# Bucketed attention and two dense blocks on one core: later bucket products and value halves for the second batch

## The chip, the core and the metric

One NeuronCore of a Trainium2 chip runs the whole program. The metric is the device time of one execution in microseconds (us), the median of several runs. TensorE (PE in the rows) does the matrix products into PSUM, VectorE (DVE), ScalarE (ACT) and GpSimd (POOL) the elementwise work, and SyncE (SP) issues all transfers that matter here, among them the transposing ones. Each engine takes its instructions in the order of its own queue.

## What is computed

Attention in which a query sees only the keys of its own bucket, and then two dense blocks on the result. Two batches of 8 heads, 768 positions, 64 channels; the blocks have 512 and 2048 channels.

```python
q_bits = (np.einsum('bhsd,dk->bhsk', q, proj) > 0)      # 6 bits each, the same for k
mask = q_bucket[:, :, :, None] == k_bucket[:, :, None, :]
scores = np.where(mask, scale * np.matmul(q, k.transpose(0, 1, 3, 2)), -1000000000.0)
attn = np.exp(scores - np.max(scores, axis=-1, keepdims=True))
attn_out = np.matmul(attn / (np.sum(attn, axis=-1, keepdims=True) + 1e-09), v)
x = attn_out.transpose(0, 2, 1, 3).reshape(B * S, H * D)
h = x @ w_in;    x = np.where(h > 0.0, h, np.exp(np.minimum(h, 0.0)) - 1.0) @ w_out
h = x @ w_in2;   out = (s * np.maximum(h, 0.0) ** 2 + b) @ w_out2
```

## The kernel before

Numbers are kept as pairs of 16-bit halves, a high one and a low one, so that each product is made of several. The attention runs in 96 **units**: unit `u` is 128 queries of one head against all 768 keys. Units 0 to 47 are the first batch, 48 to 95 the second; 8 units, one for each head, make a chunk of 128 positions, and two heads make a **pair** (0 to 3) that is prepared together. Unit 48 + 2p is the first that needs pair p of the second batch.

A unit has these steps: scores `s` on TensorE (`u_s`, L358), minimum over the row and scaling on VectorE and the exponential on ScalarE (`u_soft`, L368 to L370), the split of the probabilities into halves `ph`, by ScalarE (L389) and a subtraction on GpSimd (L392), a transposing transfer to `pt` (L394), and the product with the values, `xacc` (`u_av`, L412), some units later: `nxt["lag"]` lets the scores run five units ahead. Between the steps of the units stand the products of the first dense block, `h` and `x2p` (L531), which the outer loop deals out by a running credit. That block works on two chunks at a time, and only needs chunks that the attention has finished.

A pair of the second batch is prepared by steps that the function `attention` calls after the softmax of a given unit, from the table `sched`, in the order of the entries. For pair `p`, with `e1 = 41 + 2p`:

- `p_load` fetches k, q and v (`LOAD1`, `LOADV1`);
- `p_split` at `e1` makes the halves of k and q and issues three transposing transfers;
- `p_bits` at `e1 + 3` multiplies k and q by the projection (`pbit`, 14 small products, L320), compares with zero on VectorE (`bits`, L323) and copies a part of k (L326);
- `p_buck` at `e1 + 4` turns the bits into 64 further channels of k and q, by which a query and a key of different buckets get a very low score. For k and for q: two products `pone` on TensorE (L333) and two pieces on ScalarE, which read PSUM and write k or q (L337). Then the pair is ready;
- `p_v` at `PV1[p]` makes the halves of v: the high one on ScalarE (L303), the low one on VectorE (L304).

The second batch has for `s`, `pbit` and `pone` one pool of two PSUM tiles in turn (`NS = 2`), and for `ph`, the halves of k and q and `bits` one ring of four buffers (`NPH` and one of `EX`).

The order in this text is a priority, not the order of the queues. The framework (`TileContext` with a simulated timeline) goes through the program with times of its own and gives each engine, at each moment of that timeline, the ready instruction that was traced first. The queues it writes are then fixed: on the chip an engine waits for the next instruction of its queue even if a later one could run.

Of the kernel before, what the change touches and what calls it, by code (L numbers as in the profile page):

```python
# [41 lines left out]
WST = 2  # L42
LOAD1 = [30, 41, 42, 44]
LOADV1 = [46, 46, 48, 48]
PV1 = [48, 49, 50, 52]

GUEST = [(0, "k"), (0, "q"), (2, "k"), (2, "q"), (0, "v"), (1, "v")]
NS = 2
# [19 lines left out]
def model_kernel(tc, q, k, v, proj, w_in, w_out, w_in2, w_out2, s2, b2, sel, pop, eye, out):  # L68
# [24 lines left out]
    with ExitStack() as base:  # L93
# [350 lines left out]
        def at(step, fn, *a):  # L444
            sched.setdefault(step, []).append((fn, a))
# [10 lines left out]
        for hp in range(HP):  # L456
            at(PV0 + hp, p_v, 0, hp)
            e1 = (C - 1) * H + 2 * hp + 1
            at(LOAD1[hp], p_load, 1, hp, "k")
            at(LOAD1[hp], p_load, 1, hp, "q")  # L460
            at(e1, p_split, 1, hp, "k", "act")
            at(e1, p_split, 1, hp, "q", "act")
            at(e1 + 3, p_bits, 1, hp)
            at(e1 + 4, p_buck, 1, hp)
            at(LOADV1[hp], p_load, 1, hp, "v")
            at(PV1[hp], p_v, 1, hp)
        done_chunks = [0]
# [512 lines left out]
```

## Time and profile before

| | us |
|---|---|
| median of 3 runs (713.94 to 717.16) | 716.36 |
| profiled execution | 715.27 |
| its span, first to last instruction | 713.5 |
| TensorE matmul busy | 659.6 |
| VectorE busy | 516.6 |
| ScalarE busy | 417.2 |
| GpSimd busy | 272.7 |

Rows of time read: start in us, duration in us, engine, line, operation, output <- inputs, shape, count, and in brackets the idle time of the engine just before with what released it. `PEclk` is the clock that TensorE was granted as a share of the full one; a share of 0.50 is 1.2 GHz.

### The profile page before, as it was taken

The numbers are of one execution on the slowest core, as the hardware profiler recorded it, in microseconds if no ns is written. First come the engines' busy times: TensorE is split into PE (matmuls) and PEld (weight loads), VectorE is DVE, ScalarE is ACT, GpSimd is POOL, SyncE is SP. The second block draws the span as 40 slices with busy tenths as digits, with TensorE's granted clock in tenths as the row PEclk, the third lists the DMA queues.
The fourth block names the chain that finished last, engine by engine and source line by source line (L and its number), as shares of the span: only waits on it lengthen the run. The fifth ranks groups of instructions, "written<-read, shape, count | busy, mean of one in ns | idle before, by whom it ended". The sixth has DMA issues, their size and how long they took to land.

```text
span 713.5 us, 15214 instructions
## 1 busy us (share of the span) xinstructions
PE 659.6 (92%) x6192; PEld 504.0 (71%) x6192; DVE 516.6 (72%) x885; ACT 417.2 (58%) x687; POOL 272.7 (38%) x219
## 2 busy tenths in 40 slices
PE   2789869888887999999999999999999999999998
PEld 0368657676666777888888988874444446888887
DVE  5688899888878468645744699439999726999730
ACT  2897679874797887756755333234555525555520
POOL 1257778873445278945854421311211200000000
PEclk9999979999999999999999999999999999999999
DMA  9984599999899588966768545004453000000100
GB/s 234 259 222 135 159 223 225 205 229 219 178 208 215 88 142 159 154 119 123 123 112 120 132 153 175 1 25 125 121 149 115 0 1 1 16 30 32 45 30 30
DMA packets 206742, 89.73 MB, mean 126 GB/s; under 512 B 171856, under 2 KB 203344, under 8 KB 206672
## 3 DMA queue, kind: packets, MB, share of 16 engines
q1 hardware_dynamic: 206080, 88.63, 56.4%
q8 instruction: 48, 0.79, 0.5%
q10 hardware_dynamic: 592, 0.14, 0.1%
q14 instruction: 22, 0.18, 0.1%
HBM read 43.13 MB, written 3.15 MB: 65 GB/s over the span
## 4 chain that ended last, share of the span: by engine, by line
PE 59%; DMA 11%; ACT 10%; DVE 7%; issue 6%; POOL 5%; SPq 0%; DVEq 0%; ACTq 0%; POOLq 0%
PE h L531 24%; PE y L775 15%; PE x2p L531 10%; DMA pt<-ph 6%; PE s L358 4%; POOL ph L392 3%; ACT p L370 3%; PE xacc L412 3%; ACT ph L389 2%; PE xacc L406 1%; DVE e L546 1%; DMA k<-src 1%; ACT gh L551 1%; PE pT L379 1%; DVE p L368 1%
## 5 line engine op out<-in xcount | busy, mean ns | idle before, releaser
L392 POOL TENSOR_TENSOR ph<-p,ph 128x768 f16<-128x768 f32 x80 | 133.9, 1679 | 65.3 <-ACT ph L389 45.7
L531 PE MATMUL h<-x,wih 128*128 128x256 f16 x768 | 132.5, 276 | 0.1
L531 PE MATMUL h<-x,wi 128*128 128x512 f16 x576 | 124.5, 379 | 0.0
L368 DVE TENSOR_SCALAR_CACHE_REDUCE p<-s 128x768 f32<-128x768 f32 x96 | 91.0, 950 | 44.4 <-PE s L358 42.1
L370 ACT ACTIVATE p<-p,mx 128x768 f32<-128x768 f32 x96 | 89.1, 928 | 46.4 <-DVE mx L369 40.5
L775 PE MATMUL y<-wqh,a 128*128 128x256 f16 x672 | 110.3, 273 | 0.0
L775 PEld LDWEIGHTS <-a 128*128 128x128 f16 x1008 | 98.5, 98 | 11.8
L531 PE MATMUL x2p<-gh,woh 128*128 128x256 f16 x384 | 104.8, 274 | 2.0 <-ACT woh L188 1.0
L531 PE MATMUL x2p<-gh,wol 128*128 128x256 f16 x384 | 105.0, 274 | 1.5 <-DVE wol L204 1.5
L531 PE MATMUL h<-x,wil 128*128 128x256 f16 x384 | 106.0, 276 | 0.0
L531 PE MATMUL x2p<-gl,woh 128*128 128x256 f16 x384 | 104.9, 274 | 0.5 <-POOL gl L554 0.4
L531 PEld LDWEIGHTS <-wi 128*128 128x128 f16 x576 | 56.3, 98 | 67.8
L775 PE MATMUL y<-wql,a 128*128 128x256 f16 x336 | 91.2, 273 | 0.0
L358 PE MATMUL s<-k,q 128*128 128x512 f16 (+1 forms) x384 | 81.0, 336 | 4.8 <-DVE p L368 4.5
L531 PEld LDWEIGHTS <-woh 128*128 128x128 f16 x768 | 74.8, 98 | 13.5 <-ACT woh L188 1.4
L531 PEld LDWEIGHTS <-wih 128*128 128x128 f16 x768 | 75.2, 99 | 12.8 <-issue 0.5
L554 POOL TENSOR_TENSOR gl<-g,gh 128x512 f16<-128x512 f32 x48 | 58.1, 1211 | 63.3 <-ACT gh L551 62.7
L412 PE MATMUL xacc<-vv,pt 128*128 128x64 f16 x1440 | 57.7, 195 | 18.2 <-DMA pt<-ph 18.2
L412 PEld LDWEIGHTS <-pt 128*128 128x128 f16 x1440 | 53.9, 99 | 24.3 <-DMA pt<-ph 21.2
L389 ACT ACTIVATE ph<-p 128x768 f16<-128x768 f32 x80 | 66.6, 836 | 5.2 <-DMA pt<-ph 4.1
L567 DVE SCALAR_TENSOR_TENSOR g<-h,sbs,r 128x512 f32<-128x512 f32 x48 | 35.7, 745 | 23.6 <-ACT r L564 23.6
L564 ACT ACTIVATE r<-h 128x512 f32<-128x512 f32 x48 | 28.2, 590 | 39.5 <-PE h L531 39.5
(121 smaller groups left out, 1043.3 us busy)
## 6 DMA issues: line engine op xcount, KB each, us to landing
wraw<-in_moe_w_in SPq DMA_DIRECT2D x32, 512.0 KB, 3.8
wraw<-in_moe_w_out SPq DMA_DIRECT2D x32, 512.0 KB, 3.9
out<-y SPq DMA_DIRECT2D x10, 256.0 KB, 2.0
raw<-in_k SPq DMA_DIRECT2D x6, 384.0 KB, 4.4
raw<-in_q SPq DMA_DIRECT2D x6, 384.0 KB, 4.4
v<-in_v SPq DMA_DIRECT2D x4, 384.0 KB, 5.1
pt<-ph SPq DMA_TRANSPOSE x80, 4.0
x<-in_k SPq DMA_DIRECT2D x2, 384.0 KB, 5.0
```

Of the source, the lines that this page charges most:

```text
L358: nc.tensor.matmul(p[:, a0:a1], w[b, hp][:, j, c, :], kf[:, a0:a1], start=(x == 0), stop=(x == 1))
L368: nc.vector.tensor_scalar(f, sps.pop(u), CLAMP, None, op0=ALU.min, op1=ALU.min, accum_out=mx)
L370: nc.scalar.activation(out=f, in_=f, func=ACTF.Exp, scale=-sm / (SQ * SQ), bias=mx, accum_out=sums[b, c][:, h:h + 1])
L379: nc.tensor.transpose(p[:, 128 * cc:128 * cc + 128], f[:, 128 * cc:128 * cc + 128], ident)
L389: nc.scalar.activation(out=t[:, 0, :], in_=f, func=ACTF.Copy)
L392: nc.gpsimd.tensor_tensor(out=t[:, 1, :], in0=f, in1=t[:, 0, :], op=ALU.subtract)
L412: nc.tensor.matmul(acc, o[:, C * x + cc, :], vv[:, j, cc, y, :], start=(z == 0 and cc == 0), stop=(z == 2 and cc == C - 1))
L531: nc.tensor.matmul(p, ws[a](kk), xs[b](kk), start=(kk == 0 and z == 0), stop=(kk == n_kk - 1 and z == 2))
L554: nc.gpsimd.tensor_tensor(out=gl, in0=t["g"], in1=gh, op=ALU.subtract)
L564: nc.scalar.activation(out=t["r"], in_=p, func=ACTF.Relu, scale=UN)
L567: nc.vector.scalar_tensor_tensor(out=g, in0=p, scalar=sb["s"], in1=t["r"], op0=ALU.mult, op1=ALU.mult)
L775: nc.tensor.matmul(p, a[:, xa, kk, :], wq[y][:, WQ[n], kk, :], start=first and k == 0, stop=k == 3 * K2 - 1, skip_group_check=True)
```

## The change

The bucket products of a pair of the second batch (`p_buck`) are called two units behind its bit products, not one: at units 46, 48, 50 and 52 where it was 45, 47, 49 and 51. The halves of v (`p_v`) are made at units 48, 50, 52 and 54 where it was 48, 49, 50 and 52. Within a unit the entries keep the order of the pairs, so that unit 48 now has the halves of v of pair 0, the bucket products of pair 1 and the bit products of pair 2; unit 50 those of pairs 1, 2 and 3; unit 52 the halves of pair 2 and the bucket products of pair 3; and unit 54 the halves of pair 3. Loads, splits and bit products stay at their units.

```diff
 LOADV1 = [46, 46, 48, 48]
-PV1 = [48, 49, 50, 52]
+PV1 = [48, 50, 52, 54]
+BUCK1 = 5
...
             at(e1 + 3, p_bits, 1, hp)
-            at(e1 + 4, p_buck, 1, hp)
+            at(e1 + BUCK1, p_buck, 1, hp)
             at(LOADV1[hp], p_load, 1, hp, "v")
             at(PV1[hp], p_v, 1, hp)
```

## Rows read from the trace of the kernel before

**Rows 1.** The page: TensorE in 40 slices, and the chain that ended last

```profile
PE   2789869888887999999999999999999999999998
...
PE 59%; DMA 11%; ACT 10%; DVE 7%; issue 6%; POOL 5%; SPq 0%; DVEq 0%; ACTq 0%; POOLq 0%
```

**Rows 2.** Windows: length, busy us by engine, PEclk, DMA share, GB/s

```profile
200.00:260.00 60.00, 53.31 (x593) 41.34 (x591) 39.48 (x75) 49.66 (x79) 29.61 (x20) 0.97 0.83 159
260.00:300.00 40.00, 38.90 (x515) 32.93 (x513) 30.39 (x64) 32.42 (x59) 35.02 (x25) 1.00 1.01 161
300.00:400.00 100.00, 99.80 (x1251) 86.25 (x1250) 53.76 (x114) 59.40 (x100) 59.09 (x41) 1.00 0.68 117
400.00:714.00 314.00, 309.06 (x2262) 220.70 (x2259) 227.30 (x320) 131.90 (x207) 35.08 (x23) 1.00 0.21 65
```

**Rows 3.** Waits of TensorE, 200 to 260: total us, times, longest

```profile
PE xacc L412 <- DMA pt<-ph: 4.4, 5, 1.3
PE pone L333 <- DVE bits L323: 2.3, 1, 2.3
```

**Rows 4.** Windows around the wait for bits

```profile
228.60:230.90 2.30, 0.00 (x0) 0.00 (x0) 2.30 (x3) 0.34 (x1) 2.30 (x2) 1.00 0.53 153
230.90:234.10 3.20, 3.17 (x14) 1.89 (x14) 2.49 (x6) 0.63 (x1) 0.60 (x1) 0.50 1.12 139
234.10:240.00 5.90, 5.90 (x76) 4.62 (x74) 1.98 (x5) 5.83 (x9) 1.64 (x1) 0.98 0.20 44
```

**Rows 5.** Timeline of TensorE, 224 to 238

```profile
224.32 0.27 PE L320 MATMUL pbit<-k,pjk1l 128*32 128x256 f16 x1
...
228.33 0.27 PE L531 MATMUL x2p<-gl,woh 128*128 128x256 f16 x1
230.93 0.80 PE L333 MATMUL pone<-bits,sel_sb 128*128 128x512 f16 x2 [2.33 <-DVE bits L323]
231.52 0.42 PE L531 MATMUL x2p<-gh,wol 128*128 128x256 f16 x1
...
237.06 0.81 PE L358 MATMUL s<-k,q 128*128 128x512 f16 x4
```

**Rows 6.** Timeline of VectorE, 225 to 231

```profile
225.97 0.72 DVE L326 COPY k<-k 64x768 f16<-64x768 f16 x1 [2.07 <-DMA k<-srcl]
226.73 3.27 DVE L304 SCALAR_TENSOR_TENSOR vv<-x,vv 128x768 f16<-128x768 f32 x2
229.93 0.94 DVE L323 TENSOR_SCALAR bits<-pbit 128x768 f16<-128x768 f32 x1
```

**Rows 7.** Timeline of ScalarE, 233 to 239

```profile
233.47 0.93 ACT L370 ACTIVATE p<-p,mx 128x768 f32<-128x768 f32 x1 [4.53 <-DVE mx L369]
...
234.52 1.80 ACT L337 ACTIVATE k<-pone,pop_sb 64x768 f16<-64x768 f32 x2
...
237.09 1.80 ACT L337 ACTIVATE q<-pone,pop_sb 64x768 f16<-64x768 f32 x2
```

**Rows 8.** L304, 180 to 262: ns min/median/max; and GpSimd's timeline

```profile
L304 DVE SCALAR_TENSOR_TENSOR vv<-x,vv x2: 958/1679/2400, 226.7 to 227.6; 128x768 f16<-128x768 f32 x2
L304 DVE SCALAR_TENSOR_TENSOR vv<-raw,vv x2: 957/958/958, 232.4 to 239.7; 128x768 f16<-128x768 f32 x2
...
226.97 4.53 POOL L392 TENSOR_TENSOR ph<-p,ph 128x768 f16<-128x768 f32 x2 [0.49 <-ACT ph L389]
```

**Rows 9.** Timeline of TensorE: scores of units 52 and 54

```profile
247.13 0.81 PE L358 MATMUL s<-k,q 128*128 128x512 f16 x4
...
250.36 0.81 PE L358 MATMUL s<-k,q 128*128 128x512 f16 x4
```

**Rows 10.** Timelines: a wait of VectorE for a buffer, two of TensorE

```profile
206.43 1.43 DVE L265 SCALAR_TENSOR_TENSOR srcl<-x,src 128x384 f16<-128x384 f32 x2 [1.51 <-DMA pt<-ph]
...
219.10 0.55 PE L412 MATMUL xacc<-vv,pt 128*128 128x64 f16 x13 [1.35 <-DMA pt<-ph]
...
242.56 0.52 PE L412 MATMUL xacc<-vv,pt 128*128 128x64 f16 x12 [0.85 <-DMA pt<-ph]
```

**Rows 11.** Timeline of TensorE, first pairs, first batch

```profile
20.26 0.61 PE L320 MATMUL pbit<-k,pjkhl 128*32 128x512 f16 x2 [3.22 <-ACT k L337]
```

## The prediction

> **What bounds the kernel now.** I read the page first: TensorE is the engine with the most work, and the chain that ended last lies on it for 59% of the span [rows 1]. The reader is to see in the 40 slices that it is nearly full from about 240 us on and not before. Next the long stretches: from 300 to 400 us TensorE is idle for 0.2 of 100 us, from 400 to 714 for 4.9 of 314, most of that the tail, from 260 to 300 for 1.1 of 40, but from 200 to 260 for 6.7 of 60 [rows 2]. The change touches units 45 to 54, and these run in that stretch. So the kernel is bound by TensorE's work plus the holes in it, and a hole closed in 200 to 260 is kept, since what follows is full. A hole there needs only one cause: TensorE takes its instructions in the order of its queue, and x2p products that could run stand behind the one that waits.
>
> Then TensorE's waits of that stretch: 4.4 us in five waits for transposed probabilities (DMA), and 2.3 us in one wait for `bits` [rows 3]. The change speaks to the second. It lies at 228.60 to 230.93, and the 3.2 us behind it ran at a granted clock of 0.50, the lower of the two levels (1.2 GHz), with x2p products of 0.42 us where 0.27 is usual [rows 4, 5].
>
> Why `bits` is late is on VectorE's row. The bit products of pair 2 ended at 224.6 [rows 5], so their comparison (L323) could have run then. It stood behind the copy of pair 3 (L326), which waited 2.07 us for its transpose, and behind two low halves of values (L304, pairs 0 and 1), 3.27 us in all; it began at 229.93, and the product `pone` of pair 2 (L333) began as it ended [rows 5, 6]. Behind it came the softmax of unit 49, so ScalarE sat idle for 4.53 us until 233.47 [rows 7].
>
> **The change, part by part.** No instruction is added or taken away; each is traced later, which lowers its priority, and the planner fills the queues anew.
>
> Bucket products of pair 2, from unit 49 to unit 50. In the queue they come behind the scores of unit 50 and whatever product TensorE has for the meantime; those scores ran at 237.06, 6 us behind the first `pone` of the pair, and x2p products ran in between [rows 5]. These are what hides the move. TensorE need not stop at 228.60: the wait of 2.33 us goes, and with it 3.20 us x (1 - 0.50) = 1.6 us of clock. Sum 3.9 us. If that cover is gone (no x2p product ready), the 2.33 stay.
>
> Low half of pair 1, from unit 49 to unit 50. Of the two L304 rows the first took 0.96 us and the second 2.40; the other two pairs took 0.96 each [rows 8]. The long one is pair 1's, it ran beside GpSimd's subtraction [rows 8], and it starts when the comparison could have followed pair 0's at 227.7. Taking it out alone ends the comparison near 228.6, the moment at which TensorE stopped. So two of the moves remove the same 2.3 us, which makes the removal safer and not larger. The Trainium skill (SBUF — State Buffer, "Who interferes with whom") says that a VectorE instruction with two SBUF inputs contends with a GpSimd instruction that reads SBUF; 2.40 against 0.96 agrees. By that rule the moved instruction can meet the next unit's subtraction and lose the same 1.44 us there, ahead of another comparison, and the sum would be 1.44 smaller.
>
> Low halves of pairs 2 and 3, from 50 and 52 to 52 and 54: 0.96 us on VectorE and about as much on ScalarE each, read only by the value products of units 52 and 54, up to five units behind their scores (the code's lag). Cost nothing; if a value product did wait for one, 0.96.
>
> Bucket products of pairs 0 and 1, from 45 and 47 to 46 and 48. Their four ScalarE pieces (1.80 us for k, as much for q [rows 7], both per pair) come about a unit later. ScalarE is busy for 49.7 of 60 us [rows 2], but the hole of 4.53 us at 229 takes the 3.6 us that are pushed through it [rows 7]. Cost nothing, 3.6 us if the hole is filled first.
>
> Bucket products of pair 3, from 51 to 52. Now the scores of unit 54, which read them, come 3.2 us after those of unit 52 [rows 9]; between the two must lie one `pone` and both ScalarE pieces, 0.5 + 3.6 = 4.1 us. Unit 54 comes at least 0.9 us later. TensorE has x2p products to put there, so 0 to 0.9 on its row; I take 0 and keep the rest for the range.
>
> Held buffers. `bits` sits in the four-deep `ph` ring and in the queue of the probabilities until its product has read it, so each of the four now holds a slot for one unit longer. Its price is not in the trace. The bounds are 0 and the 1.51 us that VectorE waited for such a slot once [rows 10], twice that for the two pairs that fall in the crowded part. On TensorE this shows as longer waits for `pt`, now 1.35 and 0.85 us [rows 10]. I take one more wait of the smaller size, 0.8 us, since VectorE and ScalarE catch up by some 2 us at unit 49.
>
> Sum: 3.9 - 0.8 = 3.1 us less. No DMA is issued by the moved steps, so SyncE's queue keeps its order but for the moments at which its inputs are ready.
>
> **The rivals.** (B) The hole moves. The planner, which places instructions by its own times, ordered pair 3's copy ahead of pair 2's comparison though the chip had them the other way; it can do as badly with the new order, or leave `pone` where it was. For it: `pone` of the other three pairs waited for no comparison before, so one bad place in four is what this planner makes. Against: two independent moves remove this one. It gives 2.3 + 1.6 back: 716.4, within about 2 us.
>
> (C) The hole was also what delayed the units behind it: unit 49's softmax is some 2 to 5 us sooner, the transposes with it, and the wait of 0.85 at 242.56 and others for `pt` shrink. For it: ScalarE's hole of 4.53 us [rows 7] and the DMA engines, busy for 0.20 from 234.1 to 240 [rows 4]. The price is 3.9 + 0.85 + some of the other 3.5 us for `pt`: 5 to 8 us less, 710.5.
>
> (D) Slower. With two score buffers in PSUM, unit 50 is now followed by both `pone` tiles of pair 2 and the bit products of pair 3 with no scores between, so the bit products wait until ScalarE has read the first `pone`, and the scores of unit 51 until it has read the second. The trace shows that wait once, in the first pairs: bit products 3.22 us behind ScalarE's piece of k [rows 11]. The same at pair 3 for unit 54, 3.6 us. Both, each with 1.6 us of clock behind it, are 10 us, less the 3.9: 6 us more, 722.5. It decides where TensorE has no other product in its queue at that point, that is, if the x2p products of this block have been used up earlier. Against it: none of TensorE's waits of the stretch was for ScalarE before [rows 3].
>
> **How the numbers follow.** The profiled execution took 715.27 us, its span 713.5; the median of the runs is 716.36, 1.09 more. The forecast is 712.2 for a profiled execution and 716.36 - 3.1 = 713.3 for the median. Chances: forecast (711 to 716) 0.48, B 0.15, C 0.22, D 0.15. About 0.5%, 3.6 us, is what a measurement of this kernel can tell from no change. Of the forecast's 0.48 some 0.18 lies beyond 3.6 us (the 3.9 with nothing given back), so faster is 0.22 + 0.18 = 0.40, slower 0.15 and the same 0.45. The range runs from 708.5, C's far end, to 720.5, between D with one of its two waits (717.3) and with both (722.5); some 0.05 and 0.10 are left out.
>
> **What would show it.** Right: no wait of TensorE for `bits` over 0.5 us between 200 and 260, no stretch at 0.50 near 230, the `pone` of pair 2 behind unit 50's scores, its comparison ahead of pair 1's low half, ScalarE's hole below 2 us, TensorE idle for some 3.5 to 4.5 us in that stretch against 6.7. Wrong: a wait of TensorE for ScalarE's pieces of k or q, for scores' buffers or for `pt` of over 2 us in the same stretch, or work missing from 260 on that the stretch before had done.

## The result: slower by half a per cent

The changed kernel takes 717.59 us (median of 20 runs, 714.03 to 721.34) beside 713.87 us for the kernel before on the same chip (20 runs, 711.26 to 719.26): a ratio of 1.0052, 95% interval 1.0035 to 1.0069, or 3.7 us more. The forecast was 3.1 us less. Its line numbers are those of before plus one.

Up to the comparison of pair 0 (L324, at 195.28 us; 198.77 before) both kernels have the same instructions in the same order on VectorE, ScalarE and GpSimd; TensorE has in the changed kernel one unit's scores ahead of it, 0.65 us, that come later in the kernel before. So I measure from its start to the end of the span: 514.7 us before, 520.3 after, 5.6 more. That is one profiled execution of each; the medians say 3.7. Within this **stage** the gaps between TensorE's matmuls add up to 9.3 us before and 13.3 after, and it worked for 3.4 us at a granted clock of 0.50 before and 5.8 after. 4.0 us of idle time and half of 2.4 us of slow time make 5.2: the two account for nearly all of the 5.6.

The windows of after, with the columns of [rows 2]:

```profile
200.00:260.00 60.00, 50.75 (x573) 39.00 (x571) 37.68 (x71) 48.02 (x75) 27.37 (x19) 0.94 0.81 153
260.00:300.00 40.00, 39.27 (x507) 33.06 (x504) 31.60 (x58) 29.09 (x52) 33.21 (x23) 1.00 0.93 156
300.00:400.00 100.00, 98.23 (x1235) 84.79 (x1233) 53.35 (x116) 61.58 (x104) 57.97 (x40) 1.00 0.67 116
400.00:714.00 314.00, 310.94 (x2281) 222.76 (x2277) 229.19 (x323) 132.31 (x208) 36.33 (x24) 1.00 0.21 65
226.80:229.30 2.50, 0.07 (x2) 0.02 (x1) 2.26 (x2) 0.79 (x1) 2.42 (x2) 1.00 0.85 175
229.90:232.35 2.45, 0.01 (x1) 0.01 (x1) 2.38 (x4) 1.27 (x2) 1.17 (x1) 0.79 1.22 223
232.35:236.00 3.65, 3.65 (x17) 2.46 (x17) 0.12 (x1) 3.46 (x5) 0.00 (x0) 0.50 0.90 173
```

From 200 to 260 TensorE is idle for 9.25 us where it was 6.7 [rows 2], and the stretch from 300 to 400, full before, lacks 1.8. In the place of the one hole of 2.30 us there are two, of 2.50 and 2.45, with slow time behind the second. What TensorE waited for from 200 to 262:

```profile
PE xacc L413 <- DMA pt<-ph: 3.4, 3, 1.4
PE pone L334 <- DVE p L369: 2.5, 1, 2.5
PE x2p L532 <- POOL gl L555: 2.4, 1, 2.4
PE s L359 <- DVE bits L324: 0.6, 1, 0.6
PE x2p L532 <- DVE g L549: 0.2, 1, 0.2
```

The wait of `pone` for `bits` [rows 3] is gone, as forecast, and two of the same size have come. Their places, on TensorE:

```profile
222.65 0.81 PE L359 MATMUL s<-k,q 128*128 128x512 f16 x4
...
224.61 0.81 PE L359 MATMUL s<-k,q 128*128 128x512 f16 x4
...
226.35 0.49 PE L334 MATMUL pone<-bits,sel_sb 128*128 128x512 f16 x2
229.28 0.27 PE L532 MATMUL x2p<-gl,woh 128*128 128x256 f16 x1 [2.43 <-POOL gl L555]
...
232.34 0.80 PE L334 MATMUL pone<-bits,sel_sb 128*128 128x512 f16 x2 [2.46 <-DVE p L369]
232.93 0.42 PE L532 MATMUL x2p<-gh,wol 128*128 128x256 f16 x1
```

These are the scores of units 49 and 50 and the two `pone` products of pair 2. The **first hole** is GpSimd's queue. `gl`, the low half of the dense block's input that x2p reads, needs `gh`, which ended at 225.02 (ScalarE, below). It stood behind the subtractions of units 47 and 48, where in the kernel before it ran ahead of them (those of [rows 8], at 226.97). Before, then after:

```profile
225.32 1.16 POOL L554 TENSOR_TENSOR gl<-g,gh 128x512 f16<-128x512 f32 x1 [4.62 <-ACT gh L551]
```

```profile
223.84 3.55 POOL L393 TENSOR_TENSOR ph<-p,ph 128x768 f16<-128x768 f32 x2 [7.67 <-ACT ph L390]
227.36 1.86 POOL L555 TENSOR_TENSOR gl<-g,gh 128x512 f16<-128x512 f32 x1
```

```profile
224.40 0.62 ACT L552 ACTIVATE gh<-g 128x512 f16<-128x512 f32 x1
```

The **second hole** is VectorE's queue. The second `pone` needs the score buffer that unit 50's scores hold until VectorE has read them (L369). They were there at 225.4; VectorE read them at 231.31, behind the low half of pair 2's values and two copies of pair 3's q:

```profile
218.98 1.82 DVE L305 SCALAR_TENSOR_TENSOR vv<-x,vv 128x768 f16<-128x768 f32 x2
...
221.29 0.96 DVE L324 TENSOR_SCALAR bits<-pbit 128x768 f16<-128x768 f32 x1 [0.49 <-DMA k<-src]
...
225.78 2.42 DVE L305 SCALAR_TENSOR_TENSOR vv<-raw,vv 128x768 f16<-128x768 f32 x1 [0.43 <-ACT vv L304]
228.45 2.83 DVE L296 COPY q<-q 64x768 f16<-64x768 f16 x2 [0.24 <-DMA q<-src]
231.31 0.96 DVE L369 TENSOR_SCALAR_CACHE_REDUCE p<-s 128x768 f32<-128x768 f32 x1
```

### The profile page after: what moved, and what is told of

It reads as the page before. It is cut to its first block, busy times and chain, and to the rows that moved or that the text cites. A ratio compares the mean times of both kernels' runs of the same rounds, so it can differ in the third digit from the quotient of the medians.

```text
span 715.6 us, 15217 instructions
## 1 busy us (share of the span) xinstructions
PE 657.7 (92%) x6192; PEld 503.5 (70%) x6192; DVE 522.7 (73%) x885; ACT 417.5 (58%) x687; POOL 271.4 (38%) x219
## 4 chain that ended last, share of the span: by engine, by line
PE 63%; DMA 10%; DVE 9%; ACT 8%; issue 5%; POOL 4%; SPq 0%; DVEq 0%; ACTq 0%; POOLq 0%
PE h L532 25%; PE y L776 15%; PE x2p L532 11%; DMA pt<-ph 5%; PE s L359 4%; PE xacc L413 3%; DVE e L547 2%; POOL ph L393 2%; ACT p L371 2%; DMA k<-src 2%; PE xacc L407 2%; DVE p L369 2%; ACT ph L390 2%; DMA q<-src 2%; ACT gh L552 1%
## 5 line engine op out<-in xcount | busy, mean ns | idle before, releaser
L369 DVE TENSOR_SCALAR_CACHE_REDUCE p<-s 128x768 f32<-128x768 f32 x96 | 91.1, 952 | 39.3 <-PE s L359 35.6
L776 PEld LDWEIGHTS <-a 128*128 128x128 f16 x1008 | 98.6, 98 | 11.7
```

The source lines that it names most:

```text
L369: nc.vector.tensor_scalar(f, sps.pop(u), CLAMP, None, op0=ALU.min, op1=ALU.min, accum_out=mx)
L776: nc.tensor.matmul(p, a[:, xa, kk, :], wq[y][:, WQ[n], kk, :], start=first and k == 0, stop=k == 3 * K2 - 1, skip_group_check=True)
```

## The experiments

The theory after the result: the loss is the two holes, each made by one instruction that the planner put into another place; the rival: the loss is spread over a timeline that was planned anew, and closing a hole opens another. Two facts about the queues needed no run. With the value halves moved alone (`PV1`), the planner writes the same queues as before on every engine; with the bucket products moved alone, the same as for the whole change. So half of the change does nothing, and all of it is `BUCK1`. Each ratio below is to runs of the kernel before on the same chip.

In the diffs below, `behind(later, first)` gives the planner an order between two instructions of one engine's queue and adds no wait. Such a line moves the line numbers of the rows by up to sixteen.

**The two holes of the changed kernel, closed one by one.** First VectorE: unit 50's softmax ahead of pair 2's low half and of pair 3's q copies, which for this are called at unit 50 and not with the split.

```diff
+            if (b, hp) == (1, 2):          # low half of v, p_v
+                behind(i_, mark["soft", 50])
...
+                if (b, hp) == (1, 3):      # copies of q
+                    behind(i_, mark["soft", 50])
```

> The changed kernel with one order undone on VectorE: the low half of pair 2's values and the copies of pair 3's q are queued behind the softmax of unit 50, not ahead of it. Theory H (the loss is two holes of TensorE near 227 to 232, 2.43 us behind the last low half of g on GpSimd and 2.46 us behind unit 50's softmax, with 2.9 us of half clock behind them, 7.8 us against 3.9 before): the second hole goes and with it some of the clock, 2.5 to 3.8 us less than the changed kernel, so a ratio to the kernel before of 1.000 to 1.002; TensorE's wait of pone for VectorE's softmax is under 0.5 us. Rival R (the bucket products one unit later slow the attention as a whole, and TensorE's holes only show it): the wait closes but another of about the same length opens, ratio 1.004 to 1.007.

Ratio 1.0053 (1.0032 to 1.0074): nothing gained, as the rival had it. Then GpSimd: the block's last `gl` ahead of the subtractions of units 47 and 48.

```diff
+                if mark["gl"] == 16:
+                    behind(mark["ph", 47], i_)
+                    behind(mark["ph", 48], i_)
```

> The changed kernel with one order undone on GpSimd: the last low half of g of the second block is queued ahead of the subtractions of units 47 and 48, as it was before the change. Theory H: the hole of 2.43 us of x2p behind GpSimd goes, with 0 to 1.3 us of half clock, 2.4 to 3.7 us less than the changed kernel, ratio to the kernel before 1.000 to 1.002. Rival R: the two units' probabilities come later by the 1.2 us of that instruction, the waits for pt grow by it, ratio 1.003 to 1.007.

Ratio 0.9995 (0.9976 to 1.0014): the whole loss is gone. And both:

> Both orders undone in the changed kernel. Theory H: both holes and the half clock behind them go, 7.8 us less than the changed kernel at most, ratio to the kernel before 0.993 to 0.997. Rival R: the holes open elsewhere, ratio 1.002 to 1.007.

Ratio 0.9971 (0.9955 to 0.9987), 2.1 us less than the kernel before (the plain medians, 712.83 and 713.74, are only 0.9 apart). TensorE's timeline, of the first of the three (waits over 1 us up to 310, and the one for `gl`):

```profile
207.07 0.38 PE L427 MATMUL xacc<-vv,pt 128*128 128x64 f16 x7 [2.04 <-DMA pt<-ph]
...
231.24 0.27 PE L548 MATMUL x2p<-gl,woh 128*128 128x256 f16 x1 [0.91 <-POOL gl L571]
...
245.01 0.45 PE L427 MATMUL xacc<-vv,pt 128*128 128x64 f16 x5 [2.64 <-DMA pt<-ph]
```

of the second (waits over 1 us):

```profile
236.73 0.49 PE L339 MATMUL pone<-bits,sel_sb 128*128 128x512 f16 x2 [3.26 <-DVE p L374]
```

and of both together (the same):

```profile
208.00 0.38 PE L427 MATMUL xacc<-vv,pt 128*128 128x64 f16 x7 [1.17 <-DMA pt<-ph]
...
246.12 0.70 PE L427 MATMUL xacc<-vv,pt 128*128 128x64 f16 x18 [1.18 <-DMA pt<-ph]
```

VectorE's hole closed alone comes back as waits for `pt`. GpSimd's order alone takes x2p's wait away and leaves `pone`'s, which even grows to 3.26; still the time falls by 0.0057 of it, 4.1 us. With both no hole over 1.2 us and no slow time is left in the stage. The four kernels are a table of two by two: GpSimd's order is worth 0.0057 and 0.0082, VectorE's 0.0000 and 0.0024. Each of these differences is uncertain by some 0.0025, so GpSimd's are clear of the noise and VectorE's are not. One further trait goes with it: from 300 to 305 the changed kernel waits 0.94 us for `gh` and 0.82 for `gl`, and with `gl` ahead neither is there.

**Is `gl`'s place enough?** The opposite in the kernel before: the last `gl` behind both subtractions, the change left out.

```diff
+                if mark["gl"] == 16:
+                    behind(i_, mark["ph", 47])
+                    behind(i_, mark["ph", 48])
```

> The kernel before with one order changed on GpSimd: the last low half of g of the second block is queued behind the subtractions of units 47 and 48, two instructions of 1.64 us each. Nothing else is asked of the planner. Theory G (the order alone is the loss): x2p waits 2 to 3 us for it, with up to 1.7 us of half clock, ratio 1.003 to 1.007. Rival C (the order costs only because ScalarE's high half before it is late too, which pair 0's pieces bring): a wait under 1 us, ratio 0.999 to 1.002.

Ratio 1.0045 (1.0023 to 1.0066), the size expected, but not by the wait expected:

```profile
232.71 1.01 PE L418 MATMUL xacc<-vv,pt 128*128 128x64 f16 x18 [3.18 <-DMA pt<-ph]
...
303.48 0.27 PE L537 MATMUL x2p<-gh,woh 128*128 128x256 f16 x1 [1.00 <-ACT gh L557]
304.71 0.27 PE L537 MATMUL x2p<-gl,woh 128*128 128x256 f16 x1 [0.82 <-POOL gl L560]
```

No x2p waits for `gl` near 229. The planner, given the one order, filled all queues behind it in another way, the wait for `bits` fell to 0.34 us, and a wait of 3.18 for `pt` took its place. In this plan the place of `gl` costs this much, with all that the planner changed after it; which wait shows it depends on the rest of the plan.

**The pairs one by one.** From the kernel before, with its `PV1`; `BUCK1` becomes a list, with 5 for the pairs named and 4 for the others.

```diff
-            at(e1 + 4, p_buck, 1, hp)
+            at(e1 + BUCK1[hp], p_buck, 1, hp)
```

Pair 0 alone; its plan alone among the four has `gl` behind the two subtractions:

> The kernel before with the bucket products of pair 0 alone one unit later (unit 46); the values stay. In the planned queue of GpSimd the last low half of g of the second block stands behind the subtractions of units 47 and 48, as in the whole change. Theory G (this order, brought by pair 0, is the loss): ratio to the kernel before 1.003 to 1.007, with x2p waiting 1 to 2.5 us for that low half between 220 and 235. Rival M (the loss comes from the later pairs, whose products hold the score buffers): 0.998 to 1.002.

1.0014 (0.9994 to 1.0034). `gl` comes behind and yet nothing waits for it near 229; the waits are small ones, for `pt` (the longest 1.50) and 0.87 for a softmax. Theory G failed here: this order without the other moves is not the loss.

Pair 1 alone and pair 3 alone:

> Pair 1's bucket products alone one unit later. Theory S: the moves are priced one by one and add up; with 1.0014 for pair 0 and 1.0025 for pair 2 alone, 1.0052 for all four leaves 0.0013 for pairs 1 and 3 together, so each gives 0.999-1.002. Theory Q: each move makes the planner write other queues and the size of the loss does not follow from the pair; pairs 1 to 3 together gave 1.0033, and a single one gives anything from 0.996 to 1.005, outside S's interval for at least one of pairs 1 and 3.

> Pair 3's bucket products alone one unit later. Theory S: 0.999-1.002, as for pair 1. Theory Q: outside it for at least one of the two. The forecast's own step for this pair was 0 to 0.9 us, 1.000-1.0013, and its rival of waits for score buffers 3.6 us with 1.6 of clock behind it, 1.005-1.007, with a wait of TensorE for ScalarE's piece of k or for a score buffer of over 2 us between 240 and 255.

1.0014 (0.9996 to 1.0032) and 0.9998 (0.9980 to 1.0016). Pair 1 takes two waits (1.92 for a softmax, 1.97 for `pt`) for the one of 2.33; pair 3 keeps that one, 2.29 us, and has the 0.79 that the forecast's step for this pair allowed:

```profile
229.38 0.49 PE L334 MATMUL pone<-bits,sel_sb 128*128 128x512 f16 x2 [2.29 <-DVE bits L324]
234.84 0.81 PE L359 MATMUL s<-k,q 128*128 128x512 f16 x4 [0.79 <-ACT k L338]
```

Pair 2 alone, the forecast's main step:

> The kernel before with the bucket products of pair 2 alone one unit later (unit 50), the move of which the prediction spoke. The low halves of pairs 0 and 1 still stand ahead of the comparison in the planned queue. Theory P (TensorE has passed on to x2p products and the comparison is done when pone comes): no wait for bits, ratio 0.994 to 0.998. Rival S (pone now waits for a score buffer until unit 50's softmax has run, as in the whole change, 2.46 us there): ratio 0.999 to 1.003.

1.0025 (1.0004 to 1.0046). VectorE's rows, then TensorE's:

```profile
226.09 0.87 DVE L327 COPY k<-k 64x768 f16<-64x768 f16 x1 [1.92 <-DMA k<-srcl]
226.99 3.27 DVE L305 SCALAR_TENSOR_TENSOR vv<-x,vv 128x768 f16<-128x768 f32 x2
230.19 0.94 DVE L324 TENSOR_SCALAR bits<-pbit 128x768 f16<-128x768 f32 x1
```

```profile
231.18 1.44 PE L359 MATMUL s<-k,q 128*128 128x512 f16 x4 [2.34 <-DVE bits L324]
...
233.06 0.84 PE L334 MATMUL pone<-bits,sel_sb 128*128 128x512 f16 x2
```

`pone` comes behind the scores, as forecast, and these scores wait in its place: for the score buffer that the bit products hold until the same late comparison has read them. The hole is the same, 2.34 for 2.33, and 3.22 us at a clock of 0.50 follow it as 3.20 did [rows 4]. The comparison stands behind the same instructions as in [rows 6].

Pairs 1 to 3 together, without pair 0:

> The bucket products of pairs 1, 2 and 3 one unit later, pair 0 as before. The last low half of g stands ahead of the subtractions of units 47 and 48 in the planned queue. Theory G: no wait of x2p for it, ratio 0.994 to 1.001. Rival M: 1.003 to 1.007.

1.0033 (1.0015 to 1.0052): no wait for `gl` near 229, but waits for `pt` of 1.96 and 2.65. So there is a loss without `gl`'s order as well, and rival M's interval held in both runs. The single moves of pairs 1 and 3 lie in theory S's interval, and the four single ratios add up to 0.0051 more than one where the whole change has 0.0052. Prices that add up are not ruled out by that; but each has an uncertainty of 0.002, and each kernel waits at other places, so I read no law in it.

**The hole of the kernel before, by its cause.** Pair 3's copy and pair 1's low half queued behind pair 2's comparison, first in the kernel before:

```diff
+            if (b, hp) == (1, 3):          # copy of k, p_bits
+                behind(i_, mark["bits", 1, 2])
...
+            if (b, hp) == (1, 1):          # low half of v, p_v
+                behind(i_, mark["bits", 1, 2])
```

> The kernel before with one order changed on VectorE: the copy of pair 3 and the low half of pair 1 are queued behind the comparison of pair 2. It prices the hole that the prediction wanted to close. Theory P (that hole is worth its 2.33 us and 1.6 us of half clock): 3 to 4 us less, ratio 0.9945 to 0.996, no wait of TensorE for bits over 0.5 us. Rival W (the comparison waits for its buffer of the ph ring, which a transpose of pair 3 frees late, so that being queued first helps little; or the hole moves): ratio 0.998 to 1.003.

0.9976 (0.9958 to 0.9995), 1.7 us less. On VectorE the comparison now runs 5.2 us earlier than in [rows 6], and TensorE neither waits for it nor works at half clock in the stage; three other waits have grown:

```profile
224.74 0.95 DVE L331 TENSOR_SCALAR bits<-pbit 128x768 f16<-128x768 f32 x1
225.61 1.53 DVE L310 SCALAR_TENSOR_TENSOR vv<-x,vv 128x768 f16<-128x768 f32 x1
227.17 1.69 DVE L334 COPY k<-k 64x768 f16<-64x768 f16 x1
```

```profile
234.97 0.39 PE L328 MATMUL pbit<-k,pjkhl 128*32 128x512 f16 x2 [1.25 <-ACT q L347]
...
244.82 0.55 PE L422 MATMUL xacc<-vv,pt 128*128 128x64 f16 x13 [1.65 <-DMA pt<-ph]
...
271.64 0.70 PE L422 MATMUL xacc<-vv,pt 128*128 128x64 f16 x18 [1.22 <-DMA pt<-ph]
```

The hole was worth 2.33 + 3.4/2 = 4.0 us. In the profiled execution the slow time is gone, but TensorE's idle time fell by only 1.0, from 9.3 to 8.3: 2.7 in all. The runs say 1.7, with bounds of 0.4 and 3.0. The rest came back as other waits.

The same two lines with pair 2's bucket products moved:

> Pair 2's bucket products alone one unit later, and on VectorE pair 3's copy and pair 1's low half of the values queued behind pair 2's comparison. Theory V: the 1.44 us that the scores waited in the run of pair 2 alone, [2.34 idle], is the comparison standing behind these two instructions, the same cause as the wait of pone for bits in the kernel before. Then no wait of TensorE for bits over 0.5 us between 200 and 260 is left, and the ratio to before falls from 1.0025 to 0.997-1.000. Rival F: the scores wait for a buffer that later steps hold as well, and the wait stays (over 1 us, with another releaser); ratio 1.001-1.005.

1.0017 (0.9999 to 1.0034). (The 1.44 us in the expectation is the duration in that row; the wait was 2.34.) Theory V held for the cause: no wait for `bits` is left anywhere from 200 to 262, so the wait of the scores in the run of pair 2 alone was that comparison. Its time did not; the ratio lies in rival F's interval. Up to 260 TensorE has what the forecast wanted of its main step, no wait for `bits` and no half clock, though it is idle for 5.7 us and not for 3.5 to 4.5. Then a wait stands where none was:

```profile
265.15 1.14 PE L422 MATMUL xacc<-vv,pt 128*128 128x64 f16 x18 [2.55 <-DMA pt<-ph]
```

```profile
262.60:265.15 2.55, 0.00 (x1) 0.00 (x1) 0.07 (x1) 1.39 (x3) 2.55 (x3) 0.99 1.08 70
265.15:268.40 3.25, 3.25 (x27) 2.30 (x28) 2.00 (x5) 1.20 (x2) 2.67 (x3) 0.50 1.09 237
```

**All of it as sums.** Stage, TensorE's idle time in it and the time that it worked at half clock, us, from one profiled execution each; the last column is the stage less the idle time and half of the slow time, that is, the work and the tail of 3.1 to 3.2 us behind TensorE's last product.

| kernel | ratio | stage | idle | slow | rest |
|---|---|---|---|---|---|
| before | 1 | 514.7 | 9.3 | 3.4 | 503.7 |
| after | 1.0052 | 520.3 | 13.3 | 5.8 | 504.1 |
| after, VectorE's order | 1.0053 | 517.9 | 12.2 | 2.7 | 504.3 |
| after, GpSimd's order | 0.9995 | 513.7 | 8.8 | 3.4 | 503.2 |
| after, both orders | 0.9971 | 512.5 | 8.2 | 0.0 | 504.3 |
| before, `gl` behind | 1.0045 | 519.2 | 12.0 | 3.4 | 505.5 |
| pair 0 | 1.0014 | 515.2 | 10.8 | 0.0 | 504.4 |
| pair 1 | 1.0014 | 515.1 | 9.3 | 3.4 | 504.1 |
| pair 2 | 1.0025 | 516.3 | 10.3 | 3.3 | 504.3 |
| pair 3 | 0.9998 | 515.3 | 10.6 | 0.0 | 504.7 |
| pairs 1 to 3 | 1.0033 | 518.6 | 11.7 | 3.4 | 505.2 |
| before, comparison early | 0.9976 | 512.7 | 8.3 | 0.0 | 504.4 |
| pair 2, comparison early | 1.0017 | 515.5 | 9.9 | 3.4 | 503.9 |

The rest is alike to within 2.3 us; the order of the ratios is that of idle and slow time, but for a microsecond or two.

## Why the prediction was wrong, step by step

**What bounds the kernel.** That TensorE's row decides and that the time is its work plus its holes held in all thirteen kernels. The sentence "a hole closed in 200 to 260 is kept, since what follows is full" is the step that failed first. With the comparison early a hole of 4.0 us gave 1.7; with pair 2 moved as well the stretch after 260 got a wait of 2.55 us that was not there. A row that is full in the plan of before need not be full in a new plan.

**Bucket products of pair 2** (3.9 us less). This is the main term, and it failed: alone the move took 1.8 us more, not 3.9 less. The reading of the cause was right: the comparison late behind a copy that waits for its transpose and two low halves. The move did not act on it: it changed the instruction that waits, from `pone` to the scores, at the same 2.34 us. In the whole change the wait for `bits` did go, since the planner set the comparison ahead of pair 3's copy (221.29, then 222.88), but the cover named, x2p, stood still itself for 2.43 us. The step had said it: without that cover the 2.33 stay.

**Low half of pair 1.** Wrong: the new `PV1` changes no queue. The planner makes the half as soon as its inputs are there, ahead of the comparison, whatever unit it is called at. The argument of two moves against one cause fell with it. The 1.44 us beside GpSimd's subtraction did move on, as the Trainium skill's rule (SBUF — State Buffer, "Who interferes with whom") let one fear: pair 2's low half took 2.42 us beside the subtractions that ended at 227.4, against 0.96 before [rows 8]. It stood not ahead of a comparison but of unit 50's softmax, for which the second `pone` waits.

**Low halves of pairs 2 and 3** (nothing). Pair 2's came earlier, not later: 225.78 against 232.4 at the earliest [rows 8]. With the q copies it is the second hole.

**Bucket products of pairs 0 and 1** (nothing). This term was put at nothing from ScalarE's row alone, the 3.6 us per pair. `gh` does come later there, 29.1 us after the start of the stage where it was 25.9, but not too late: it ended at 225.02, `gl` takes 1.16 us, and TensorE stopped at 226.84. What made the hole was GpSimd's queue, which none of the steps looked at: `gl` behind the subtractions of units 47 and 48, 3.55 us. In the plan of the whole change the removal of that order gave back 4.1 us. It is no price of the order by itself: pair 0's move alone brings the same order at 1.0014 and with no wait for `gl`, and pairs 1 to 3 lose 0.0033 without it.

**Pair 3** (0 to 0.9). Right as far as the run can tell: 0.79 us in the trace of that move alone, and a ratio of 0.9998.

**Held buffers** (0.8). Waits for `pt` in 200 to 260 fell in the whole change, 3.4 for 4.4, and rose in others (pairs 1 to 3: 6.5). No run prices a held buffer by itself, so the 0.8 stays unshown; what the traces show is that each plan has its own waits for `pt`.

**The rivals.** B, the hole moves, is what happened, and in the run of pair 2 to the letter; its price of 3.9 us given back took for granted that one hole remains one. C: no run came near the 5 to 8 us of it. D had the right resource, two score buffers, with the wrong holder: `pone` waits 2.46 us for scores that VectorE reads late, not for ScalarE's piece, whose waits measured 0.79 (pair 3) and 1.22 (pair 2 with the comparison early) where 3.2 to 3.6 was set down. That wait of `pone` for a softmax goes with the move: it stands in the runs of pair 0, 1, 2 and pairs 1 to 3 as well (0.87, 1.92, 0.78 and 1.71 us), and not from 200 to 260 in the kernel before. B and D together had 0.30 and deserved more.

**Signs named.** No wait for `bits` over 0.5: 0.6, nearly. `pone` behind unit 50's scores: yes. No stretch at 0.50 near 230: wrong, 3.65 us and more behind the second hole. The comparison ahead of pair 1's low half: wrong, that half ran at 218.98 to 220.80 and the comparison at 221.29. ScalarE's hole below 2 us: wrong, the longest from 200 to 260 is 2.88, though it was 4.53. Idle 3.5 to 4.5 in 200 to 260: wrong, 9.25. The sign against it, a wait for score buffers of over 2 us and work missing from 260 on, is there.

**What stays open.** Why the plan with `gl` behind the subtractions also waits near 303 us was not followed to its start; GpSimd itself waits there for ScalarE's `gh` (2.07 us in the changed kernel, 0.28 with `gl` ahead), so that wait comes out of ScalarE's queue. And every order given to the planner changes its later choices, so the 4.1 us are those of `gl`'s place with all that the planner does after it, not of one wait alone.

## What to carry to other kernels

Where a planner writes fixed queues, a step moved by one unit is a new plan for every engine, so price the queues of all engines that feed the bound one (here GpSimd's, which the diff does not name) and compare the two plans before trusting any term. A late instruction is mended where it is late, by giving its place in its own queue, and not by moving the one that waits: the next user of the same buffer waits in its place. And of a closed hole in a tightly planned stretch do not count the whole: here it was 1.7 us (0.4 to 3.0) of 4.0.

## What the hardware showed beside it

The half clock does not follow from the length of a hole alone. Pair 3's move kept a hole of 2.29 us and ran at full clock behind it; in the run of pair 2 a hole of 2.34 us was followed by 3.2 us at 0.50 (1.2 GHz). In that of pair 1 a hole of 1.97 us was followed by 0.75 us at the full clock and then by 3.4 us at 0.50. Pair 3's windows, then pair 1's:

```profile
227.08:229.38 2.30, 0.02 (x1) 0.00 (x0) 2.30 (x3) 0.00 (x0) 2.30 (x2) 1.00 0.43 117
229.38:233.00 3.62, 3.62 (x32) 3.03 (x32) 2.47 (x6) 1.05 (x3) 0.58 (x1) 1.00 1.08 134
```

```profile
224.00:225.97 1.97, 0.00 (x1) 0.01 (x1) 0.00 (x0) 1.76 (x2) 0.61 (x1) 1.00 1.04 231
226.72:230.13 3.41, 3.41 (x19) 2.41 (x17) 3.38 (x4) 1.73 (x3) 3.18 (x2) 0.50 0.28 97
```

Nor does it follow from the plan. Ahead of the stage, where their queues are still the same, all thirteen kernels have a hole of 1.97 to 2.02 us in which bit products wait for k. In the profiled executions of four of them (after, after with both orders, before with the comparison early, pairs 1 to 3) a stretch at 0.50 came behind it, in the other nine none. The kernel before, whose hole ended at 186.63, then the one with the comparison early, whose hole ended at 186.71:

```profile
187.70:191.10 3.40, 3.40 (x33) 2.93 (x30) 3.37 (x6) 3.40 (x7) 3.34 (x4) 1.00 1.03 239
```

```profile
187.80:191.21 3.41, 3.41 (x19) 2.42 (x17) 3.38 (x6) 3.41 (x7) 3.35 (x4) 0.50 1.07 240
```

So the 1.6 us of clock that I put behind each hole is a price that a hole of this length pays in one execution and not in another, and the slow column of the table above is that of one execution.
